# The activation that loads the exponential's table writes into the first tile of v

## The chip, the cores and the metric

One core of a Trainium2 chip runs the whole program. The metric is the device time of one execution in microseconds; the figure for a kernel is the median of its runs. For the kernel before, three runs gave 844.75, 844.85 and 845.06 us.

The engines are named as the profile names them: PE (TensorE: matmuls and transposes, with its weight loads as PEld), DVE (VectorE), ACT (ScalarE), POOL (GpSimd) and SP (SyncE, which here only issues DMAs). ACT and POOL issue DMAs too. Each engine works through its own queue of instructions in order.

## The reference, cut to what matters

The program computes attention within blocks of 64 positions and then a feed-forward layer. q, k and v have 8 batches, 8 heads, 576 positions and 64 channels; the feed-forward weights come as 64-bit numbers.

```python
# q, k, v: (8, 8, 576, 64); w_in: (512, 2048); w_out: (2048, 512)
scores = q_c @ k_c.T / sqrt(64)            # per head, per chunk of 64 positions
attn = exp(scores - max(scores))
attn = attn / (sum(attn) + 1e-9)
x = (attn @ v_c), heads side by side       # (4608, 512)
h = x @ w_in
g = relu(h) ** 2
out = g @ w_out                            # (4608, 512)
```

## The kernel before, in words

The 4608 rows are 36 pairs of chunks, 128 rows each. They are cut into feed-forward blocks of 4, 4, 6, 6, 6, 6 and 4 pairs. The first four pairs (0 to 3) are the lead: their attention runs at the very start, before any feed-forward matmul. Everything later (the attention of the other pairs, the conversion of the weights from 64-bit numbers to pairs of 32-bit ones, the combinations of weights) is laid between the matmuls of the feed-forward blocks.

What the start does, in the order of the queues:

- SP and ACT load q and k of the lead's pairs. `load` (L1193) issues two DMAs of 128 KB for q and two for k of each pair; k of pairs 0 and 1 goes by ACT's queue, all else by SP's. They land in slots of the pool `const` that later hold weights (`load_one`, L231), as pieces of 256 bytes in each partition.
- POOL makes the identity matrix `ident` (L1186) and then issues the loads of v for pairs 0 to 3, four DMAs of 64 KB each (`load_lead_v`, L261, into the tiles `vn`), sixteen in all.
- DVE sets a part of `qt` to zero, and PE multiplies it with itself 17 times (`heat`, L1001), with no use made of the result.
- ACT, behind its four k issues, runs an activation with the function Exp on one column of `ident` (L1195). In front of it stands the load of the exponential's table. Its output is one column of a tile `warm`, 128 bytes of each partition, that nothing reads.
- For each pair PE transposes q and k (L427), ACT or DVE copies them out of PSUM (L436, L441), PE multiplies them (L449), DVE takes the maximum and subtracts it (L456, L460), ACT takes the exponential (L465), DVE sums (L469) and adds 1e-9 (L472; POOL does this small addition for pairs 1 and 2), DVE inverts and multiplies (L475, L476), PE transposes (L487), ACT copies (L492), PE multiplies with v (L501), and ACT and DVE write the two parts of x (L512, L514). Between these PE runs a few filling matmuls on `ident` (L395).
- SP then loads the weights, and ACT and DVE convert them (L161 to L199). The first feed-forward matmuls (L611) need all four pairs' x and the first weights.

The order on every engine is written out by a planner in the code (`class Plan`). Each operation is entered with `add`: its engine, an assumed cost, what it reads, what it writes, and for some a `line`, whose operations keep their order. The planner runs a small model of the machine in which an operation starts when what it needs is done, and the instructions are issued by the start times of that model. Within it a v load costs POOL 4 x 0.58 us, its data need 2.18 us at the assumed rate, and 0.7 us pass until it is there. The framework then puts in the waits between engines, from the tiles that the instructions read and write.

SBUF is handed out in the order of the code. In `const` the identity (512 bytes of each partition) is followed by `warm` (128 bytes) and then by the weight slots of 4096 bytes; the other pools lie behind `const`.

Of the kernel before, what the change touches and what calls it, by code (L numbers as in the profile page):

```python
# [10 lines left out]
F32 = mybir.dt.float32  # L11
# [3 lines left out]
AF = mybir.ActivationFunctionType  # L15
# [5 lines left out]
def kernel(  # L21
# [20 lines left out]
    nc = tc.nc  # L42
# [3 lines left out]
    P = 128  # L46
# [37 lines left out]
    const = ctx.enter_context(tc.tile_pool(name="const", bufs=1))  # L84
# [19 lines left out]
    early = ctx.enter_context(ExitStack())  # L104

    ident = const.tile([P, P], F32, name="ident")
    warm = const.tile([P, 32], F32, name="warm")[:, :1]


    nat = early.enter_context(tc.tile_pool(name="nat", bufs=1))  # L110
# [1 line left out]
    vn = [nat.tile([P, H // 2, 2, D], F32, name=f"vn{n}") for n in range(blocks[0])]  # L112
# [426 lines left out]
    def snap(i):  # L539

        at = 2 * NCC * HN + i * HN
        return aside()[:, at:at + HN]
# [136 lines left out]
    class Mixed(Step):  # L679
# [31 lines left out]
        def add(self, i, h, side, s):  # L711
            n = self.hn
            nc.vector.tensor_tensor(  # L713
                self.kept(i)[:, h * n:(h + 1) * n], sides[side][:, :n], snap(s)[:, :n], op=ALU.add
            )
# [88 lines left out]
    PE, DVE, ACT, SP, POOL = E.PE, E.DVE, E.Activation, E.SP, E.Pool  # L804
# [182 lines left out]
    def program():  # L987
# [4 lines left out]
        add = p.add  # L992
# [20 lines left out]
        def load(u):  # L1013
            for n, h in itertools.product(range(2), repeat=2):
                load_half(u, n, h, ACT if n and u < 2 else SP)
# [176 lines left out]
        for u in range(lead):  # L1192
            load(u)  # L1193
            if u == 1:
                add(ACT, 1.3, lambda: nc.scalar.activation(warm, ident[:, :1], AF.Exp), ["ident"], [], line="act")  # L1195
        for f, n in [(1, 0), (0, 0), (1, 1), (0, 1), (1, 2), (0, 2), (1, 3), (0, 3)]:
            (load_values if f else fetch)(n)
        for u in range(lead):
# [272 lines left out]
    with tc.manual_schedule(engines={PE, DVE, ACT, SP, POOL}):  # L1471
        program()
# [31 lines left out]
```

## Time and profile before

| | |
|---|---|
| runs of the kernel | 844.75, 844.85, 845.06 us (median 844.85) |
| the profiled execution's own time | 844.75 us |
| its span in the profile | 843.0 us |
| PE busy | 836.2 us, 99% of the span |
| PEld, DVE, ACT, POOL busy | 731.0, 546.0, 359.4, 278.1 us |
| granted TensorE clock, mean | 1.0 of full speed |
| DMA traffic | 147.42 MB, 175 GB/s in the mean |

The span runs from the first to the last instruction that the profiler saw on the core; the execution's own time has a little more around it. A line number is that of the kernel before. An engine's busy time counts its instructions' durations, not the time in which it waits or issues DMAs (POOL's issues are shown as busy). The chain of waits is followed back from the last instruction: at each step to what released it, or to the instruction ahead of it on its engine. The DMA shares are those of sixteen DMA engines; records of packets overlap, so that shares can add up to more than one. Of the DMA queues q0 is POOL's, q1 SP's and q10 ACT's.

### The profile page before, as it was taken

The page shows a single profiled execution, that of the slowest core. Times are in us where ns is not written, and L with a number is a line of the kernel's source. Part 1 is how long each engine was busy: PE and PEld are TensorE (multiplying, and loading weights), DVE is VectorE, ACT ScalarE, POOL GpSimd, SP SyncE. Part 2 cuts the span into 40 slices and gives each one's busy share as a digit, 9 for nine tenths or more (in the row PEclk, how much of TensorE's full clock was granted, in tenths as well). Part 3 has the DMA queues.
Part 4 walks back from the last instruction along what each step waited for, and adds up shares of the span by engine and source line. Part 5 has one row for each costly group of instructions (what it writes and reads, how often), then busy time and mean ns, then how long its engine had stood idle before and what let it go on. Part 6 is the DMA issues. An engine that isn't in the chain of part 4 may idle for free.

```text
span 843.0 us, 16933 instructions
## 1 busy us (share of the span) xinstructions
PE 836.2 (99%) x6259; PEld 731.0 (87%) x6259; DVE 546.0 (65%) x962; ACT 359.4 (43%) x670; POOL 278.1 (33%) x500
## 2 busy tenths in 40 slices
PE   8999999999999999999999999999999999999998
PEld 7888888878889888898998898889889989988996
DVE  5999997889765666756556846655765642463333
ACT  5898885555533233433332532333433332332222
POOL 5002546434334342243343233434313412323320
PEclk9999999999999999999999999999999999999999
DMA  9799659877498866486687568667846653548651
GB/s 292 235 275 323 152 127 295 201 166 180 119 223 172 191 161 148 105 251 152 143 186 178 130 175 203 151 144 173 189 118 183 155 133 87 141 125 236 173 151 51
DMA packets 245729, 147.42 MB, mean 175 GB/s; under 512 B 182544, under 2 KB 197136, under 8 KB 245648
## 3 DMA queue, kind: packets, MB, share of 16 engines
q0 software_dynamic: 55936, 96.50, 42.3%
q1 hardware_dynamic: 187456, 49.20, 26.6%
q8 instruction: 50, 0.82, 0.4%
q10 hardware_dynamic: 2256, 0.66, 0.3%
q14 instruction: 31, 0.25, 0.1%
HBM read 118.49 MB, written 24.12 MB: 169 GB/s over the span
## 4 chain that ended last, share of the span: by engine, by line
PE 99%; DMA 0%; DVE 0%; ACT 0%; issue 0%; ACTq 0%
PE o L741 37%; PE side L703 33%; PE h L611 11%; PE o L647 11%; PE side L346 2%; PE side L299 2%; PE side L501 1%; PE sc L449 1%; PE side L449 1%; DMA qk_raw<-in_k_dram 0%; PE side L427 0%; PE k L427 0%; PE side L487 0%; PE xt L501 0%; PE xt L395 0%; PE q L427 0%
## 5 line engine op out<-in xcount | busy, mean ns | idle before, releaser
L703 PE MATMUL side<-xc,ring 128*128 128x384 f32 (+1 forms) x1680 | 286.5, 326 | 0.0
L703 PEld LDWEIGHTS side<-xc,ring 128*128 128x128 f32 x1680 | 280.4, 188 | 6.0 <-ACT gf L718 0.3
L693 POOL DMA_DIRECT2D ring<-combos x280 | 152.0, 543 | 358.4 <-PE side L703 353.2
L713 DVE TENSOR_TENSOR gf<-side,aside 128x384 f32<-128x384 f32 (+1 forms) x120 | 63.7, 531 | 202.7 <-PE side L703 201.7
L741 PE MATMUL o<-wo,gs_f 128*128 128x512 f32 x672 | 169.8, 396 | 0.0
L741 PE MATMUL o<-wo,gs_s 128*128 128x512 f32 x672 | 159.4, 390 | 0.0
L741 PEld LDWEIGHTS o<-wo,gs_s 128*128 128x128 f32 x672 | 125.6, 188 | 26.0 <-DVE gs_s L731 0.4
L741 PEld LDWEIGHTS o<-wo,gs_f 128*128 128x128 f32 x672 | 122.6, 188 | 23.5
L709 ACT COPY aside<-side 128x384 f32<-128x384 f32 (+1 forms) x120 | 55.1, 459 | 138.4 <-PE side L703 138.0
L647 PE MATMUL o<-wo,gs 128*128 128x512 f32 x384 | 95.9, 393 | 0.0
L611 PE MATMUL h<-x,wi 128*128 128x512 f32 x384 | 95.8, 394 | 0.0
L273 POOL DMA_DIRECT2D v_raw<-in_v_dram x112 | 69.8, 635 | 67.5 <-PE side L346 55.2
L611 PEld LDWEIGHTS h<-x,wi 128*128 128x128 f32 x384 | 70.9, 188 | 14.9
L647 PEld LDWEIGHTS o<-wo,gs 128*128 128x128 f32 x384 | 71.0, 188 | 14.6
L722 DVE SCALAR_TENSOR_TENSOR gf<-gf 128x768 f32<-128x768 f32 (+1 forms) x80 | 69.4, 899 | 1.1 <-ACT gf L718 0.4
L718 ACT ACTIVATE gf<-side 128x384 f32<-128x384 f32 (+1 forms) x40 | 18.8, 471 | 76.8 <-PE side L703 76.8
L306 DVE TENSOR_REDUCE m<-side 128x4 f32<-128x256 f32 x56 | 21.1, 419 | 37.7 <-ACT aside L358 34.1
L358 ACT COPY aside<-side 128x256 f32<-128x256 f32 x56 | 18.3, 377 | 62.9 <-PE side L299 59.9
L731 DVE TENSOR_TENSOR gs_f<-gf,gs_f 128x768 fp32r<-128x768 f32 (+1 forms) x40 | 35.3, 883 | 15.1 <-ACT gs_f L726 15.0
L335 ACT COPY p<-et 128x512 f32<-128x512 f32 x28 | 17.4, 621 | 61.3 <-DVE et L329 61.3
L726 ACT CAST gs_f<-gf 128x768 fp32r<-128x768 f32 (+1 forms) x40 | 31.3, 783 | 15.6 <-PE o L741 10.3
L731 DVE TENSOR_TENSOR gs_s<-gf,gs_s 128x768 fp32r<-128x768 f32 (+1 forms) x40 | 35.8, 895 | 3.3 <-ACT gs_s L726 3.3
(106 smaller groups left out, 810.3 us busy)
## 6 DMA issues: line engine op xcount, KB each, us to landing
ring<-combos POOLq DMA_DIRECT2D x280, 256.0 KB, 3.7
wiraw<-in_moe_w_in_dram SPq DMA_DIRECT2D x16, 512.0 KB, 5.7
woraw<-in_moe_w_out_dram SPq DMA_DIRECT2D x16, 512.0 KB, 6.8
out_dram<-ob SPq DMA_DIRECT2D x32, 256.0 KB, 3.6
q_raw<-in_q_dram SPq DMA_DIRECT2D x224, 32.0 KB, 2.2
k_raw<-in_k_dram SPq DMA_DIRECT2D x224, 32.0 KB, 3.7
v_raw<-in_v_dram POOLq DMA_DIRECT2D x112, 64.0 KB, 2.5
combos<-wi POOLq DMA_DIRECT2D x48, 128.0 KB, 2.5
```

Source lines behind the costliest of these rows:

```text
L273: nc.gpsimd.dma_start(out=t[r, c], in_=s.rearrange("h j d -> j h d"))
L306: nc.vector.tensor_reduce(self.m[:, c], four[c][:, 0], axis=AX.X, op=ALU.max)
L611: nc.tensor.matmul(self.h[:, :self.n], a[:, c], bb[:, c, :self.n], start=c == 0 and i == 0, stop=last,)
L647: nc.tensor.matmul(acc[b, j], a[:, j * P:(j + 1) * P], bb, start=f == 0 and i == 0, stop=f == NF - 1 and i == 2,)
L693: nc.gpsimd.dma_start(out=ring(self.m + i).rearrange("p l c n -> p (l c n)"), in_=combos[self.p, i])
L703: nc.tensor.matmul(sides[side][:, :self.hn], w[:, l, c], part(x, r, self.hn)[:, c], skip_group_check=True, start=(c, u) == (0, 0) and i in ...
L709: nc.scalar.copy(snap(i)[:, :self.hn], sides[side][:, :self.hn])
L713: nc.vector.tensor_tensor(self.kept(i)[:, h * n:(h + 1) * n], sides[side][:, :n], snap(s)[:, :n], op=ALU.add)
L722: nc.vector.scalar_tensor_tensor(t, t, 0.0, t, op0=ALU.max, op1=ALU.mult)
L726: nc.scalar.copy(split_g(i)[0][:, :n], self.kept(i)[:, :n])
L731: nc.vector.tensor_tensor(l, self.kept(i)[:, :n], h.bitcast(F32), op=ALU.subtract)
L741: nc.tensor.matmul(acc[b, j], a[:, j * P:(j + 1) * P], bb, start=first and u == 0, stop=last and u == 2)
```

## The change

The tile `warm` is gone. The activation writes its one column into the first column of `vn[0]`, the tile of pair 0's v, which the loads of v overwrite afterwards. In the planner the operation now counts as a writer of pair 0's v, so that the loads of v, which write the same tile, come after it.

```diff
@@ -104,7 +104,6 @@
     ident = const.tile([P, P], F32, name="ident")
-    warm = const.tile([P, 32], F32, name="warm")[:, :1]
@@ -1192,7 +1191,8 @@
         for u in range(lead):
             load(u)
             if u == 1:
-                add(ACT, 1.3, lambda: nc.scalar.activation(warm, ident[:, :1], AF.Exp), ["ident"], [], line="act")
+                add(ACT, 1.3, lambda: nc.scalar.activation(vn[0][:, 0, 0, :1], ident[:, :1], AF.Exp), ["ident"], [("v", 0)],
+                    line="act")
```

## Rows read from the trace of the kernel before

**Rows 1.** The page: span, and the chain that ended last by engine.

```profile
span 843.0 us, 16933 instructions
...
PE 99%; DMA 0%; DVE 0%; ACT 0%; issue 0%; ACTq 0%
```

**Rows 2.** PE's waits, 0 to 27 us: total us, times, longest.

```profile
PE side L1001 <- DVE qt L1189: 1.0, 1, 1.0
PE side L501 <- ACT ne L465: 0.6, 1, 0.6
PE k L427 <- DMA qk_raw<-in_k_dram: 0.5, 1, 0.5
PE sc L449 <- DVE qt L436: 0.4, 1, 0.4
```

**Rows 3.** Busy time by stretches: length, PE, PEld, DVE, ACT, POOL, clock, DMA, GB/s.

```profile
27.00:240.00 213.00, 213.00 (x1564) 175.09 (x1563) 188.95 (x369) 148.77 (x284) 76.51 (x137) 1.00 0.79 208
240.00:838.00 598.00, 598.00 (x4328) 535.10 (x4327) 338.83 (x559) 194.11 (x359) 190.46 (x340) 1.00 0.65 158
```

**Rows 4.** The chain in order of time, 0 to 45 us: start, us, what.

```profile
1.25 4.01 DMA qk_raw<-in_k_dram
...
5.39 1.09 PE k L427 x4
...
27.53 4.14 PE h L611 x18
```

**Rows 5.** Timeline, 0 to 22 us: start, us, engine, line, operation, idle before.

```profile
0.72 2.22 ACTq L231 DMA_DIRECT2D qk_raw<-in_k_dram  x4
...
1.04 3.81 PE L1001 MATMUL side<-qt 128*128 128x256 bf16 x17 [1.04 <-DVE qt L1189]
1.47 10.31 POOL L261 DMA_DIRECT2D vn<-in_v_dram  x16 [0.17 <-issue]
...
4.27 0.20 ACT L1195 ACTIVATE warm<-ident 128x1 f32<-128x1 f32 x1
...
12.80 0.60 PE L427 MATMUL q<-ident,qk_raw 128*128 128x128 f32 x4
...
16.05 0.23 POOL L472 TENSOR_SCALAR nz<-nz 128x8 f32<-128x8 f32 x1 [4.28 <-DVE nz L469]
...
17.00 1.10 PE L501 MATMUL side<-tt,vn 64*64 64x64 f32 x32
```

**Rows 6.** The tile vn, 0 to 32 us: duration ns min/median/max, and landing times.

```profile
L261 POOL DMA_DIRECT2D vn<-in_v_dram x16: 615/642/794, 1.5 to 11.2; - x16
...
DMA to landing us min/median/max: 2.4/4.5/6.2
```

**Rows 7.** Timeline, 21.9 to 42 us: pair 3's matmuls with v.

```profile
25.41 1.15 PE L501 MATMUL xt<-tt,vn 64*64 64x64 f32 x32
```

**Rows 8.** DMA, 3 to 5.26 us: queue, packets, MB, share of sixteen engines.

```profile
q10 hardware_dynamic: 1054, 0.26, 51.6%
q1 hardware_dynamic: 1007, 0.25, 49.3%
q0 software_dynamic: 33, 0.07, 12.5%
```

**Rows 9.** DMA issues, 7.7 to 8.1 us: size, us from issue to landing.

```profile
qk_raw<-in_q_dram SPq DMA_DIRECT2D x1, 128.0 KB, 4.5
```

**Rows 10.** Timeline of SP, 4 to 8 us: pair 3's second q issue.

```profile
7.74 0.75 SPq L231 DMA_DIRECT2D qk_raw<-in_q_dram  x1
```

**Rows 11.** DMA by queue, 1.9 to 12.3 us.

```profile
q1 hardware_dynamic: 6234, 1.56, 68.9%
q0 software_dynamic: 422, 0.88, 25.1%
q10 hardware_dynamic: 2112, 0.52, 22.5%
```

**Rows 12.** DMA by queue, 250 to 258 us.

```profile
q1 hardware_dynamic: 1788, 0.22, 19.1%
```

## The prediction

> **What bounds the kernel now.** I read the page's span and chain first: of 843.0 us the chain that ends last lies 99% on PE [rows 1]. So the first question is where PE waits at all. The list of PE's waits in the first 27 us has four entries, 1.0, 0.6, 0.5 and 0.4 us, together 2.5 us [rows 2]. After that the table by stretches shows PE busy for 213.00 of 213.00 us and for 598.00 of 598.00 us, at the full granted clock [rows 3]. Nothing after the lead can therefore come earlier or later through PE's idle time: what an edit in the first microseconds is worth is the shift of the first long run of feed-forward matmuls (L611, at 27.53 in the chain), and that shift arrives whole at the end unless something else falls behind.
>
> The chain inside the lead begins with a transfer: the second half of pair 0's k, issued at 1.25, on the way for 4.01 us, landed at 5.26. Behind it come pair 0's transposes at 5.39 and then link after link to L611 [rows 4]. PE had nothing to do between the end of the heating matmuls (1.04 + 3.81 = 4.85) and 5.39; this is the 0.5 us wait for the k transfer [rows 2, 5]. The edit sits right there: the v loads that it holds back share the DMA engines with that k.
>
> **The change part by part.**
>
> *The activation.* It stays where it is on ACT's queue, behind the four k issues, with the same input column. Only its output address differs, so I cost it at zero; it ends at 4.27 + 0.20 = 4.47 [rows 5]. ACT's next work waits for pair 0's transposes, later than 5.39, and covers even a longer one by 0.9 us.
>
> *The wait on POOL.* The sixteen v issues run from 1.47 for 10.31 us [rows 5], 642 ns each in the median [rows 6]. The first of them now waits for the activation, to about 4.5; POOL works in order, so the fifteen behind it wait too. All move by 4.5 - 1.47 = 3.0 us, and the last issue ends at 4.5 + 10.3 = 14.8. Behind them on POOL stand only the two small additions of 1e-9 for pairs 1 and 2, the first at 16.05 [rows 5]. It waits for DVE, so POOL has 1.2 us to spare, 0.9 us if the lead comes 0.3 us earlier: no cost. If that cover went, the lateness would go one for one into DVE's reciprocal behind it.
>
> *Who needs v.* A v load lands between 2.4 and 6.2 us after its issue [rows 6]. Pair 0's fourth issue leaves at about 4.5 + 3 x 0.64 = 6.4 and is there by 12.6 at the latest; its first user on PE stands at 17.00 [rows 5]. Pair 3's last leaves at 14.2 and is there by 20.4; its user stands at 25.41 [rows 7]. With at least 4 us over at both ends, and the two pairs between them on the same 2.6 us step, the cost is zero.
>
> *The written order.* The planner counts the activation done at 0.8 + 4 x 0.58 + 1.3 = 4.42, so its first v is there at 4.46 + 2.32 + 2.18 + 0.7 = 9.7 and its fourth at 16.6, where it had 6.5 and 13.5 (constants of the code). The values of pairs 0 and 3, which wait for more than v, stand later than that if the plan runs near the trace (17.00 and 25.41). I take the order on PE, ACT, DVE and SP as unchanged.
>
> *What the k load gets.* From 3.0 to 5.26 us the v queue (q0) held 12.5% of the sixteen engines' time, beside 51.6% of ACT's queue and 49.3% of SP's; the sum is over one because records overlap [rows 8]. Taken out, this is 0.125 x 2.26 = 0.28 us. Bounds: none of it reaches k if SP's queue takes it all (gain 0); no more than 0.54 us can be won, for PE is busy heating until 4.85 and began the transposes at 5.39. I take 0.28, the row's own figure. A loss is not excluded, for the reason under the second rival.
>
> *What follows pair 0.* The other q and k loads, on SP, stand in front of or beside the same v traffic. With v moved 3 us back, up to any moment less v has been carried than before, so they should land no later; pair 3's q landed at 7.74 + 4.5 = 12.24 and was taken at 12.80 [rows 5, 9, 10]. Nothing else is late next, and the 0.28 us goes through.
>
> *The removed tile.* It is 128 bytes of each partition, and it stood between the identity and the weight slots. Every tile behind it moves down by 128 bytes. In the program as built before, all those large tiles begin at multiples of 256 bytes; afterwards none of them does. For the compute engines I take nothing. For the transfers no row shows an unaligned one; the nearest rows are pieces of 128 bytes, and they bound it in the second rival. I put zero in the sum, since the number of pieces stays.
>
> **Sum.** The profiled execution: 843.0 - 0.28 = 842.7 us of span. It took 844.75 us in all, 1.75 more than its span, and the median of the three runs is 844.85; less 0.28, that is 844.57, and I write 844.6. Of 844.85 us this is 0.03%; about 0.2%, or 1.7 us, is what a measurement of this kernel can tell from no change.
>
> **Rivals.**
>
> *Nothing moves at all (844.85).* The freed share goes to SP's queue, whose records hold as much of the engines as ACT's in that stretch, and k lands at 5.26 as before. For it: 49.3% against 51.6% [rows 8]. Against it: both queues' loads belong to pairs 0 and 1, and pair 0's q stands first on SP's.
>
> *The lead's loads get slower (the other side).* Place: the 256-byte pieces of q and k, which before fill one 256-byte block of SBUF and afterwards straddle two. Price: from 1.9 to 12.3 us they took (0.689 + 0.225) x 10.4 x 16 us over 6234 + 2112 packets, 18.2 ns each [rows 11]; a 128-byte piece in the late loads took 0.191 x 8 x 16 us over 1788, 13.7 ns [rows 12]. So two halves cost at most 27.3 ns, 50% more, and at least nothing. For pair 0's k, some 3.0 us of transfer since 1.9 beside v: at 50% it lands 1.5 - 0.28 = 1.2 us later. The sharper place is pair 3's q: of the 10.34 us up to its landing, 91.4 parts of 116.5 are q and k, 8.1 us, so it comes 4.05 us later, less 3.0 x 0.215 = 0.65 us for the v not yet carried, at 15.6 instead of 12.80: 2.8 us late, 847.7 us. It passes 1.7 us when a piece costs 36% more; up to 9% the forecast's gain of 0.28 us is only eaten; between, 844.9 to 846.5. For it: these loads run with the engines full. Against it: bytes and pieces stay the same, and v's own and the weights' larger packets have more bytes per piece.
>
> The Trainium skill speaks for this rival (DMA: Bandwidth & Descriptors, How a descriptor splits into AXI transactions): a piece that does not begin on a 256-byte boundary is cut at it, so one transaction becomes two. The page states it for reads, with no time; here the unaligned side is the one written, and no row of this trace shows such a piece.
>
> *POOL is late for pair 1's addition.* If each v issue took 0.06 us more, the last would end at 15.8 and the reserve of 0.9 us would be gone; to lose 1.7 us each would have to take 0.16 us more, 25%. Against it: issues of 615 to 794 ns in the trace, beside DVE work of the same kind [rows 6]. The Trainium skill has a rule that would do it (SBUF — State Buffer, in the passage on DVE blocking DMA): descriptors of POOL's DMAs wait while DVE holds a shared port, and 620 ns become about 3100. By that one such block would end the issues near 17.3, 1.5 us past the reserve, and give 844.57 + 1.5 = 846.1. The trace's longest issue, 794 ns, speaks against it.
>
> *v late at the values.* It would need transfers over 10 us; the longest here was 6.2 [rows 6]. Then 844.9 and up.
>
> **How the numbers follow.** Forecast (0.1 to 0.5 us earlier) 0.42; nothing moves 0.28; slower loads 0.18, of it 0.10 below 1.7 us and 0.08 above; POOL late 0.06, of it 0.02 above; v late 0.02; a plan that comes out in another order 0.04, half of it faster by more than 0.2%. On the lead's own terms a faster verdict is out of reach: even all of PE's waits but the first 1.0 us make 1.5 us [rows 2]. Faster 0.02, within 0.2% 0.88, slower 0.10. The range goes from the greatest gain, 844.85 - 0.54 = 844.3, to loads 28% slower, where pair 3's q is 8.1 x 0.28 - 0.65 - 0.56 = 1.05 us late: 845.9.
>
> **What would show it.** Right: POOL's first v issue after the activation's end, the second half of k landing near 5.0, the transposes at 5.1, L611 0.3 us earlier, no new PE wait, and the additions of POOL at their places behind DVE. Wrong: a time per q or k packet well over 18.2 ns, PE waiting for q or k of pairs 1 to 3, POOL still issuing at 16, or the order on PE changed.

## The result, and the profile after

The changed kernel takes 849.22 us (median of six runs, 848.41 to 849.90), the kernel before 844.65 us (six runs, 843.99 to 845.06). The ratio is 1.0054, with a 95% interval of 1.0042 to 1.0066: 4.6 us slower, where 0.3 us faster was forecast and 845.9 us was the upper end of the range.

The profiled execution of the changed kernel took 849.63 us, its span 847.9 us against 843.0 [rows 1]. Line numbers are one lower than before. First the list of what PE waited for, 0 to 32 us (us in total, times, longest):

```profile
PE side L500 <- ACT tt L491: 2.3, 1, 2.3
...
PE k L426 <- DMA qk_raw<-in_k_dram: 0.9, 2, 0.6
PE q L426 <- DMA qk_raw<-in_q_dram: 0.9, 1, 0.9
...
```

Against [rows 2] three waits are new: 0.9 us for a q, 0.36 us for a second k, and 2.3 us for ACT. The timeline shows them in order (start, us, engine, line, operation, idle before):

```profile
4.77 5.74 POOL L260 DMA_DIRECT2D vn<-in_v_dram  x9 [3.47 <-ACT vn L1194]
...
5.42 0.82 PE L426 MATMUL k<-ident,qk_raw 128*128 128x128 f32 x4 [0.57 <-DMA qk_raw<-in_k_dram]
...
7.55 1.15 PE L448 MATMUL sc<-kt,qt 64*64 64x64 f32 x32 [0.44 <-DVE qt L435]
...
13.55 0.63 PE L426 MATMUL q<-ident,qk_raw 128*128 128x128 f32 x4 [0.85 <-DMA qk_raw<-in_q_dram]
...
15.62 0.63 PE L426 MATMUL k<-ident,qk_raw 128*128 128x128 f32 x4 [0.36 <-DMA qk_raw<-in_k_dram]
...
18.03 1.10 PE L500 MATMUL side<-tt,vn 64*64 64x64 f32 x32
...
19.66 0.67 ACT L160 ACTIVATE wia<-wiraw 128x512 f32<-128x512 f32 x1 [2.30 <-DMA wiraw<-in_moe_w_in_dram]
...
22.86 1.98 PE L500 MATMUL side<-tt,vn 64*64 64x64 f32 x32 [2.27 <-ACT tt L491]
...
27.18 1.15 PE L500 MATMUL xt<-tt,vn 64*64 64x64 f32 x32
...
31.60 4.39 PE L610 MATMUL h<-x,wi 128*128 128x512 f32 x18
```

The same places of the kernel before are these:

```profile
7.81 1.15 PE L449 MATMUL sc<-kt,qt 64*64 64x64 f32 x32 [0.44 <-DVE qt L436]
...
20.11 1.15 PE L501 MATMUL side<-tt,vn 64*64 64x64 f32 x32 [0.55 <-ACT ne L465]
...
22.87 1.15 PE L501 MATMUL xt<-tt,vn 64*64 64x64 f32 x32
...
27.29 4.38 PE L611 MATMUL h<-x,wi 128*128 128x512 f32 x18
```

From the two lists the lateness can be read off step by step. Pair 0's scores stand 0.26 us earlier (7.55 against 7.81). That is not k's doing, whose transposes start at 5.42 against 5.39: they ran slowly for a shorter time, and the trace's record of the full clock begins at 5.83 us here, at 6.40 before. Pair 0's matmuls with v stand 1.03 us later (18.03 against 17.00 in [rows 5]), so pair 3's q and k cost 1.29 us. Pair 1's are 2.75 us later (22.86 against 20.11): 1.72 us more, from ACT, which stood 2.30 us until the first weights landed, with the other pairs' work queued behind it. Pair 2's are 4.31 us later (27.18 against 22.87): 1.56 us more, from a PE that ran slowly after its wait (1.98 us for the 32 matmuls instead of 1.15). Feed-forward starts 4.31 us later, and 0.6 us more of the span's 4.9 comes afterwards, which I did not follow.

The slow stretch is in the table by stretches (us, busy time of PE, PEld, DVE, ACT, POOL, granted clock, DMA share, GB/s). Three rows of the changed kernel's lead, and the clock from 23 to 26 us:

```profile
4.00:8.00 4.00, 3.00 (x31) 2.19 (x31) 0.69 (x1) 1.04 (x3) 3.23 (x5) 1.00 1.30 221
8.00:12.00 4.00, 4.00 (x76) 3.63 (x72) 2.30 (x5) 2.12 (x4) 3.46 (x7) 1.00 1.30 202
12.00:16.00 4.00, 2.79 (x46) 2.25 (x46) 2.73 (x6) 1.70 (x3) 3.23 (x6) 1.00 1.17 230
23.00:26.00 3.00, 3.00 (x38) 2.75 (x38) 2.93 (x7) 1.73 (x4) 0.00 (x0) 0.50 1.04 374
```

The kernel before in the same stretches:

```profile
4.00:8.00 4.00, 3.02 (x22) 2.21 (x22) 0.69 (x1) 1.05 (x3) 3.84 (x8) 1.00 1.18 297
8.00:12.00 4.00, 4.00 (x82) 3.70 (x79) 2.13 (x4) 2.12 (x4) 3.64 (x6) 1.00 1.23 298
12.00:16.00 4.00, 3.92 (x60) 3.29 (x56) 3.53 (x8) 2.56 (x5) 0.00 (x0) 1.00 1.08 326
```

The engines of the DMA are as full as before (share 1.30 against 1.18 and 1.23), yet they move 202 to 230 GB/s instead of 297 to 326. So the engines do not stand idle: each piece takes longer. Against [rows 11] the queues show it too, 1.9 to 12.3 us (packets, MB, share of sixteen engines):

```profile
q1 hardware_dynamic: 5367, 1.33, 80.3%
q10 hardware_dynamic: 2112, 0.52, 26.6%
q0 software_dynamic: 184, 0.39, 17.8%
```

That is (0.803 + 0.266) x 10.4 x 16 us over 7479 packets, 23.8 ns each instead of 18.2.

Theory A: the 128 bytes that the change takes out of each partition push every tile off the multiples of 256 bytes, and the lead's transfers pay for it. Theory B, its rival: v's traffic, moved 3 us back, slows what SP loads beside it.

### The profile page after: what moved, and what is told of

Its sections match the earlier page's. It is cut to its first block, busy times and chain, and to the rows that moved or that the text cites. A ratio compares the mean times of both kernels' runs of the same rounds, so it can differ in the third digit from the quotient of the medians.

```text
span 847.9 us, 16934 instructions
## 1 busy us (share of the span) xinstructions
PE 838.0 (99%) x6259; PEld 732.2 (86%) x6259; DVE 546.3 (64%) x962; ACT 359.5 (42%) x670; POOL 278.6 (33%) x500
## 4 chain that ended last, share of the span: by engine, by line
PE 97%; DMA 2%; SPq 0%; ACT 0%; issue 0%; ACTq 0%; DVE 0%
PE o L740 37%; PE side L702 33%; PE h L610 11%; PE o L646 11%; PE side L345 2%; PE side L298 2%; DMA wiraw<-in_moe_w_in_dram 1%; PE side L500 1%; DMA qk_raw<-in_k_dram 1%; PE side L448 1%; PE side L426 0%; SPq L230 0%; PE xt L394 0%; PE xt L500 0%; PE side L486 0%; PE pt L486 0%
## 5 line engine op out<-in xcount | busy, mean ns | idle before, releaser
L740 PE MATMUL o<-wo,gs_f 128*128 128x512 f32 x672 | 169.8, 396 | 0.0
L740 PE MATMUL o<-wo,gs_s 128*128 128x512 f32 x672 | 159.3, 390 | 0.0
L740 PEld LDWEIGHTS o<-wo,gs_s 128*128 128x128 f32 x672 | 125.6, 188 | 26.0 <-DVE gs_s L730 0.4
L740 PEld LDWEIGHTS o<-wo,gs_f 128*128 128x128 f32 x672 | 122.5, 188 | 23.4
L610 PE MATMUL h<-x,wi 128*128 128x512 f32 x384 | 95.8, 394 | 0.0
L610 PEld LDWEIGHTS h<-x,wi 128*128 128x128 f32 x384 | 70.9, 188 | 14.9 <-DVE wi L198 0.2
```

The costliest lines, as they stand in the source:

```text
L610: nc.tensor.matmul(self.h[:, :self.n], a[:, c], bb[:, c, :self.n], start=c == 0 and i == 0, stop=last,)
L740: nc.tensor.matmul(acc[b, j], a[:, j * P:(j + 1) * P], bb, start=first and u == 0, stop=last and u == 2)
```

## The experiments

**The wait without the shift.** The 128 bytes stay as an unused tile.

```diff
     ident = const.tile([P, P], F32, name="ident")
+    const.tile([P, 32], F32, name="pad")
```

> The changed kernel with the 128 bytes behind the identity kept as an unused tile, so that all tiles lie where they lay before and only the wait of v's loads is left. Theory A (the shift of the tiles by 128 bytes makes the lead's transfers slower; the wait is worth a small gain at pair 0): 844.4 us, 0.3 below the kernel before, with q and k packets near the 18 ns of before and PE waiting for no q or k of pair 3. Theory B (v's traffic, moved 3 us later, slows what SP loads beside it): 849 us like the changed kernel, with pair 3's q taken near 13.5 us and the first weights landing near 19.6 us.

Measured: 845.46 us (eleven runs, 844.67 to 848.58) against 844.66 of before; ratio 1.0010, interval 1.0000 to 1.0021. The loss of 4.6 us is gone, and B with it. The small gain did not come either. In its profile (span 843.0 us) pair 0's transposes no longer wait for k:

```profile
1.04 3.81 PE side L1001 x17
...
4.90 1.09 PE k L427 x4
5.99 0.87 PE q L427 x4
```

The chain goes straight from the heating matmuls into the transposes at 4.90, 0.49 us earlier than before [rows 4]. But these eight now run slowly to their end, 6.86 instead of 6.95 (the record of the full clock begins at 6.91, before at 6.40), and feed-forward begins at 27.19, 0.10 us earlier. Its rates are those of before:

```profile
4.00:8.00 4.00, 3.62 (x25) 2.71 (x25) 0.69 (x1) 1.03 (x3) 3.24 (x6) 1.00 1.25 292
8.00:12.00 4.00, 4.00 (x81) 3.63 (x76) 2.23 (x4) 2.11 (x4) 4.00 (x8) 1.00 1.11 302
```

**The shift without the wait.** In the kernel before, the activation's own tile moves behind v's.

```diff
-    warm = const.tile([P, 32], F32, name="warm")[:, :1]
...
     vn = [nat.tile([P, H // 2, 2, D], F32, name=f"vn{n}") for n in range(blocks[0])]
+    warm = nat.tile([P, 32], F32, name="warm")[:, :1]
```

> The kernel before with its 128-byte tile moved behind v's tiles: the activation still writes a tile of its own and v's loads wait for nothing, but the slots, v's tiles and nearly all others lie 128 bytes lower, as in the changed kernel. Theory A: 849 us or a little more, slow from the first microseconds on, packets of q and k near 25 ns or above, the first weights landing at 19 us or later. Theory B: 844.7 us, as before.

Measured: 850.66 us (849.31 to 851.39), ratio 1.0069, interval 1.0056 to 1.0083, with 212, 209 and 211 GB/s in the three stretches:

```profile
4.00:8.00 4.00, 2.93 (x35) 2.12 (x35) 0.69 (x1) 1.03 (x3) 3.19 (x6) 1.00 1.27 212
8.00:12.00 4.00, 3.01 (x42) 2.43 (x39) 2.07 (x4) 1.65 (x4) 3.07 (x5) 1.00 1.29 209
...
20.00:23.00 3.00, 3.00 (x55) 2.41 (x55) 1.70 (x4) 2.63 (x5) 0.00 (x0) 0.68 1.08 369
```

Here PE waits for q and k themselves, the longest time 1.96 us for pair 3's k, and the granted clock falls behind that wait, too:

```profile
18.60 1.09 PE L427 MATMUL k<-ident,qk_raw 128*128 128x128 f32 x4 [1.96 <-DMA qk_raw<-in_k_dram]
```

The shift alone makes the loss, as A says. Whether v's wait then helps or costs is open: the interval of the changed kernel, 1.0042 to 1.0066, overlaps this one.

**Which tiles.** Two kernels put only a part off the multiples of 256, each with the wait. First only the slots (q, k and the weights): 128 bytes more in the unused tile behind them.

```diff
-    att.tile([P, 32], F32, name="edge")
+    att.tile([P, 64], F32, name="edge")
```

> The changed kernel with 128 bytes more in the unused tile in front of the second pool: only the slots (q and k of the lead, the weights as loaded) lie off the multiples of 256 bytes, v's tiles and the rest on them. Theory A with the cost in the 256-byte pieces of q and k: 848 to 849 us, nearly all of the loss. Theory A with the cost in v's pieces, or in what the engines read and write: 844.5 us. Theory B: 849 us, too, so this run speaks only beside the one with the wait alone.

Second only v and what lies behind the slots: that unused tile taken out, and the pad of the first experiment.

```diff
-    att.tile([P, 32], F32, name="edge")
...
     ident = const.tile([P, P], F32, name="ident")
+    const.tile([P, 32], F32, name="pad")
```

> The changed kernel with the 128 bytes behind the identity kept and the unused tile in front of the second pool taken out: the slots lie on multiples of 256 bytes, v's tiles and all tiles behind the slots 128 bytes off. Theory A with the cost in q's and k's pieces: 844.5 to 845 us. With the cost in v's pieces: up to 849 us. Theory B: 849 us.

Measured: 854.30 us (ratio 1.0116, interval 1.0102 to 1.0130) and 853.96 us (1.0110, 1.0096 to 1.0124). Both are slower than either of the kernels with everything in step, which no theory expected. Feed-forward begins at 28.36 and 28.14 us, about 1 us late each, against 27.19 with nothing off and 31.60 with all off. In the slots' kernel this is as A has it: 221 GB/s between 4 and 8 us, and PE waits 0.70 us for pair 3's q. The other kernel moves 289 GB/s and PE waits for no q or k; there the chain of the lead runs over POOL, and DVE waits for it:

```profile
9.22 7.08 DMA vn<-in_v_dram
...
16.58 0.62 POOL vn L260
...
17.27 0.24 POOL nz L471
```

```profile
DVE nz L474 <- POOL nz L471: 1.4, 1, 1.4
```

POOL's last v issue stood until an earlier v load had landed, and the addition for pair 1 behind it came 1.4 us late for DVE. Whether v's offset made that landing late is not shown.

The further 8.6 and 8.0 us of span come behind the lead, in PE itself (groups of the slots' kernel by line and form: busy us, mean ns):

```profile
L740 PE MATMUL o<-wo,gs_s 128*128 128x512 f32 x672 | 163.1, 395 | 0.0
...
L610 PE MATMUL h<-x,wi 128*128 128x512 f32 x384 | 97.5, 398 | 0.0
```

and the same groups of the kernel before:

```profile
L741 PE MATMUL o<-wo,gs_s 128*128 128x512 f32 x672 | 159.4, 390 | 0.0
...
L611 PE MATMUL h<-x,wi 128*128 128x512 f32 x384 | 95.8, 394 | 0.0
```

The changed kernel, with all tiles 128 bytes off, has 390 and 394 ns there. One large group did not slow in the slots' kernel: L740 with gs_f, where both operands lie in slots, took 395 ns (396 before).

**Only q and k off.** 128 bytes are left free behind the first four slots.

```diff
             pairs[pair] = {"q": t[:, 0], "k": t[:, 1]}
+            if pair == blocks[0] - 1:
+                const.tile([P, 32], F32, name="pad")
```

> The changed kernel with 128 bytes left free behind the first four slots: only these (the lead's q and k, and later four of the 32 weight tiles) lie off the multiples of 256 bytes; the other weights, v and the rest lie on them; v's loads still wait. If the 256-byte pieces of q and k carry the slowing: some 220 GB/s between 4 and 8 us instead of 280 to 305, pair 3's q taken late by 0.6 us or more, feed-forward from 28 us or later. If the loss needs v's and the weights' pieces off as well: feed-forward from 27.2 to 27.6 us. Behind the lead four of 32 weight tiles then have another offset than the tiles they are multiplied with, which by the runs with the slots alone may add an eighth of 8.6 us, about 1 us, to the total.

Measured: 848.36 us (847.98 to 849.29), ratio 1.0044, interval 1.0032 to 1.0057; 240 and 236 GB/s from 4 to 12 us; feed-forward from 28.49. So with q and k alone off the lead is 1.2 us late, and this execution lost 846.6 - 28.49 - (843.0 - 27.29) = 2.4 us behind the lead, more than the 1 us that I had reckoned for four tiles. Here, where part of the slots are off against the others, the matmuls on gs_f did slow: 398 ns, 171.1 us in all instead of 169.8. Of the runs with a part of the tiles off none lost more than 1.2 us in the lead, each by a single execution; the 4.3 us came with q, k, v and the weights off together.

**Another offset.** 64 bytes instead of none behind the identity: all tiles 192 bytes off.

```diff
     ident = const.tile([P, P], F32, name="ident")
+    const.tile([P, 16], F32, name="pad")
```

> The changed kernel with 64 bytes put behind the identity: all tiles lie 192 bytes off the multiples of 256 instead of 128. If what counts is that a 256-byte piece straddles two blocks of 256: 848.5 to 850.5 us, with 200 to 225 GB/s between 4 and 12 us. If 128 bytes off were special (two halves of equal size, or one place of the memory): nearer to 845 us, or clearly above 850.

Measured: 850.18 us (848.07 to 852.25), ratio 1.0073, interval 1.0057 to 1.0088; 222 GB/s from 4 to 8 us, 195 from 8 to 12. So a cut into two halves is not what it takes: at 192 bytes off, where the parts are unequal, the pieces are slow, too.

**256 bytes up.**

```diff
-    warm = const.tile([P, 32], F32, name="warm")[:, :1]
+    warm = const.tile([P, 96], F32, name="warm")[:, :1]
```

> The kernel before with its unused-output tile widened from 128 to 384 bytes, so that everything behind the identity lies 256 bytes higher and still on multiples of 256. If the offset within 256 bytes is what counts: 844.7 us, as before, with 290 to 300 GB/s between 4 and 12 us. If any other place than the one of before is slow (a larger period, 512 bytes, or the absolute place): 847 us or more.

Measured: 844.42 us against 844.37, ratio 1.0003, interval 0.9994 to 1.0012; 306 and 298 GB/s. 256 bytes higher cost nothing; of the four places tried, the two on multiples of 256 bytes are fast and the two off them slow.

**The stall on ACT.** In the changed kernel the first step of the first weights' conversion is ordered behind pair 1's copy.

```diff
-            add(ACT, ONE, x.keep_p, [bp] + r, ["tt"])
+            add(ACT, ONE, x.keep_p, [bp] + r, ["tt"] + ["tt1"] * (u == 1))
...
-            add(ACT, 0.66, words, [("raw", n)], [a])
+            add(ACT, 0.66, words, [("raw", n)] + ["tt1"] * (n == 0), [a])
```

> The changed kernel in which the first step of the first weights' conversion on ACT is put behind pair 1's copy of its transposed weights instead of ahead of it, so that ACT no longer stands at the first weights' landing with pair 1's and pair 2's work behind it. If that stall is what carries the lateness into PE (1.7 us of wait, 1.56 us of lower clock): pair 1's matmuls with v at about 20.5 us, no granted clock under 1.0, feed-forward from about 28.7 us, 846.3 us in all. If q and k of pair 3 and v bound the lead by themselves: 848 to 849 us.

Measured: 847.26 us (846.92 to 847.67), ratio 1.0030, interval 1.0018 to 1.0041, 2.0 us below the changed kernel where 2.9 were expected. PE's longest wait for ACT is 0.3 us, and feed-forward begins at 28.01 instead of 31.60. Not all of that is the stall: in this execution pair 3's q was taken at 12.70 instead of 13.55 and pair 0's matmuls with v stood at 17.37 instead of 18.03, both ahead of the moved step, and the planner also put pair 2's transposes (L486) ahead of pair 1's matmuls with v. What is missing came back behind the lead, among it a new wait of 0.5 us for pair 4's q:

```profile
PE side L426 <- DMA qk_raw<-in_q_dram: 0.5, 1, 0.5
```

**PE's wait and its clock, a miss.** Sixteen more matmuls on the identity in front of pair 1's matmuls with v in the changed kernel.

```diff
             self.xt = self.room("xt")
+            if self.u == 1:
+                self.fill("xt", 16)
```

> The changed kernel with sixteen more matmuls on the identity (some 1.75 us of PE) ahead of pair 1's matmuls with v, where PE stands idle for 2.27 us; their result is overwritten. If the fall of the granted clock after that wait (0.50 from 23 to 26 us) costs 1.56 us of the loss: the clock stays at full speed there, pair 1's 32 matmuls take 1.1 us instead of 1.98, and the time is 847.7 us, 1.5 below the changed kernel. If the slow stretch comes from something else (operands that arrive late, the place in SBUF): 849.2 us or above.

Measured: 849.65 us (848.43 to 850.55). It says nothing on the clock. The bank of the added matmuls is also that of pair 0's result, so they waited for DVE and began at 23.16, when pair 1's weights had been copied by 22.46; and in this execution the 2.27 us wait was not there to be filled: the start had gone slowly, and the first weights had landed when ACT came to them:

```profile
5.52 1.09 PE L426 MATMUL k<-ident,qk_raw 128*128 128x128 f32 x4 [0.66 <-DMA qk_raw<-in_k_dram]
...
8.33 1.96 PE L448 MATMUL sc<-kt,qt 64*64 64x64 f32 x32
```

PE also stood in the middle of pair 0's matmuls with v, for a reason that the profile does not show:

```profile
PE side L502 <- issue: 1.5, 1, 1.5
```

A packet of 16 KB on the instruction queue ended at 19.24 us, 1.4 us before PE went on at 20.63. In the runs with only v off and with 192 bytes PE stops at the same matmul for 0.61 and 0.70 us and goes on 1.5 us after such a packet. That PE waited for its code is not shown.

**The wait by itself.** In the kernel before, with every tile in place, the copy in front of pair 1's matmuls with v is written six times.

```diff
-            nc.scalar.copy(self.t, self.pt)
+            for _ in range(6 if self.u == 1 else 1):
+                nc.scalar.copy(self.t, self.pt)
```

> The kernel before, all tiles in place, with pair 1's copy of its transposed weights on ACT written six times instead of once, which puts pair 1's matmuls with v some 1.9 us later and leaves PE idle for about 2.4 us there, as the changed kernel has it for another reason. If the wait lowers the granted clock behind it: 0.50 for some 3 us, pair 1's 32 matmuls near 2 us, and 848.2 us in all (1.9 of delay and 1.5 of clock). If the clock of the changed kernel fell for another reason: 846.6 us, the delay alone.

Measured: 848.39 us (847.16 to 850.12), ratio 1.0049, interval 1.0037 to 1.0062, where 848.2 stood for a fall of the clock and 846.6 for none. PE stood idle for 3.46 us, and behind it:

```profile
22.16 1.98 PE L502 MATMUL side<-tt,vn 64*64 64x64 f32 x32 [3.46 <-ACT tt L493]
...
26.43 1.15 PE L502 MATMUL xt<-tt,vn 64*64 64x64 f32 x32
```

The granted clock there is the lower level, 1.2 of 2.4 GHz:

```profile
23.00:24.00 1.00, 1.00 (x22) 0.94 (x18) 0.97 (x4) 0.75 (x2) 0.00 (x0) 0.50 1.04 359
24.00:25.00 1.00, 1.00 (x9) 0.88 (x6) 0.96 (x3) 0.59 (x1) 0.00 (x0) 0.50 1.21 280
```

So the clock falls after such a wait with all tiles in place, and pair 1's 32 matmuls take 1.98 us, as in the changed kernel; from them to pair 2's it is 4.27 us instead of 2.76, 1.51 us more. These rows decide, and not the time: the wait came out 2.9 us longer than before (3.46 against 0.55) where 1.9 had been reckoned, and this execution's lead was 0.87 us ahead at pair 0's scores (6.94 against 7.81), so that 848.2 was hit in part by luck.

## Why the prediction was wrong

*What bounds the kernel.* Right: PE has no wait behind the lead after the change either, and nearly all of the loss (4.3 of 4.9 us of span) stands before the first L610.

*The activation, the wait on POOL, v's landing, the written order.* Right in the changed kernel, though the road was not all as reckoned. The first v issue stands at 4.77 (4.5 had been reckoned, and 3.0 us of delay became 3.3), POOL's addition for pair 1 ran behind DVE, no matmul with v was seen waiting for a v transfer in the changed kernel, and the instructions of PE, DVE, ACT and SP keep their order. With the shift taken out, these four cost nothing clear: ratio 1.0010, interval from 1.0000.

*What the k load gets (0.28 us).* The direction was right, the size and its worth were not. With the tiles in place PE began 0.49 us earlier, close to the upper bound of 0.54, but 0.39 of it were lost in transposes that ran at a slow rate, for the full clock came no earlier than before (6.91 against 6.40). I had taken an earlier start as an earlier end.

*The removed tile: here the sum failed.* I put zero for the transfers, "since the number of pieces stays", and gave the case above 1.7 us a chance of 0.08. Zero for the compute engines came out right, but by luck: all the tiles moved together, and with the slots alone off the matmuls lost some 8 us. Zero for the transfers was wrong. Taking 4 to 6 us, where only 256-byte pieces of q and k were on the way, the kernel with the wait alone moved 1142 + 1104 packets and the changed one 803 + 956:

```profile
q10 hardware_dynamic: 1142, 0.28, 63.2%
q1 hardware_dynamic: 1104, 0.27, 61.1%
```

```profile
q1 hardware_dynamic: 956, 0.24, 67.4%
q10 hardware_dynamic: 803, 0.20, 57.6%
```

2 x 16 us over 2246 and over 1759 are 14.2 and 18.2 ns of engine time for a piece. By the queues' shares, the measure of the prediction's 18.2 ns beside v, it is 17.7 and 22.7 ns. Either way it is 28% more, inside the bounds of nothing and 50% that the rival had from the 128-byte pieces. The rule of the Trainium skill that stood beside it (DMA: Bandwidth & Descriptors, How a descriptor splits into AXI transactions) agrees in direction, now also for the written side, which the page does not state; the runs give the price.

*The rival on the other side: mechanism right, price too small.* For 28% it said that pair 3's q would be 1.05 us late. It was taken 0.75 us late (13.55 against 12.80), and with the k behind it pair 0's matmuls with v stood 1.03 us late. But there the working stopped, with 845.9 us. What failed is "nothing else is late next". Behind q and k on SP's queue come the first weights. Their transfer took 9.6 us from the issue, before the change 5.5:

```profile
wiraw<-in_moe_w_in_dram SPq DMA_DIRECT2D x1, 512.0 KB, 9.6
```

```profile
wiraw<-in_moe_w_in_dram SPq DMA_DIRECT2D x1, 512.0 KB, 5.5
```

ACT takes them in the written order ahead of the exponentials and copies of pairs 1 and 2, so it stood 2.30 us, PE stood 2.27 us, and the clock behind that wait cost 1.56 us more. The links have their runs: with the stall removed, and the order changed with it, 2.0 us came back, and the wait alone brought the clock down. The range ended at a place that was late, not at the end of what was queued behind it.

*The other rivals.* POOL late and v late at the values: not seen in the changed kernel. POOL's sixteen issues ended at 16.1 where 14.8 had been reckoned, because three of them stood for an earlier v load to land (0.38, 0.34 and 0.31 us), yet the addition at 16.69 still waited 0.56 us for DVE. The prediction had set the issues end to end and left that wait out. With the tiles in place POOL kept 0.66 us in hand; with v off and the slots in place it was late, by 1.4 us. So this rival was near, by another road than the one that it priced.

## What to carry to other kernels

A tile that nothing reads can still be what holds its neighbours in place: when an edit adds or removes one, work out the start of every tile behind it modulo 256 bytes, for the transfers and for both operands of the matmuls. When a transfer may come late, do not stop at its first taker: follow every queue on which something stands behind it, price the last of them, and add what an idle PE costs after the wait. And an earlier start of an engine is a gain only if the engine is then at full rate.

## What the runs showed of the hardware that was not expected

- A piece of 256 bytes written into SBUF off a multiple of 256 took 18.2 ns of a DMA engine's time instead of 14.2 (at 128 bytes off, from 4 to 6 us); at 192 bytes off the lead moved 195 to 222 GB/s, at 0 (also 256 bytes higher) 292 to 306.
- Matmuls got slower when the tiles of the slots and the others were 128 bytes apart modulo 256, whichever of them was the one off: 394 to 398 ns for L611 and 390 to 395 ns for L741 on gs_s, 8.6 us over the kernel. With all off by the same 128 bytes there was no such loss, and the matmuls on gs_f, with both operands in slots, slowed only where the slots were off against each other (398 ns against 395 and 396). That the offset of a matmul's two operands from each other makes it is argued from this; why is open.
- The time at which PE reaches full rate in the start differs between executions. The trace's records of the full clock begin at 5.83 us in the changed kernel and at 10.15 us in the run with sixteen more matmuls, whose instructions are the same up to pair 1's matmuls with v; where the trace holds no record, the column of the table shows 1.00. Pair 0's 32 score matmuls took 1.15 us at 7.55 in the one and 1.96 us at 8.33 in the other, as long as the 1.98 us at a granted 0.50. Single profiles of this lead can thus differ by more than a microsecond with the same instructions, and the kernel with 256 bytes more, where the records begin at 5.40 against 6.40, began feed-forward at 26.61 instead of 27.29.
- POOL's v issues can stand until an earlier v load has landed: with the wait alone one of the sixteen did (0.51 us), in the changed kernel three, in the run with only v off the last two for 0.96 and 1.44 us.
